# Routed experts in fp32: two plain layers against seven-product block multiplication with the next expert's first layer ahead

## The chip, the cores and the metric

The kernel runs on one core of a Trainium2 chip. The metric is the device time of one execution in microseconds (us). It is the median of three runs, 475.67 us for the kernel before (475.49 to 475.71). Engines are called PE (TensorE matmul), PEld (TensorE weight load), DVE (VectorE), ACT (ScalarE), POOL (GpSimd) and SP (SyncE, which issues the weight loads).

## What is computed

A recurrent attention block gives a 384-vector for each of 3072 tokens. A router picks one of eight experts per token, and each expert is a two-layer network on its own tokens:

```python
for e in range(E):                       # E = 8
    mask = expert_idx == e
    h = np.maximum(x[mask] @ w1[e], 0.0) # w1[e]: 384 x 1024
    out[mask] = gate_w[mask, None] * (h @ w2[e])   # w2[e]: 1024 x 384
```

Everything is float32. The change is in these two products; attention and routing stay as they are.

## The kernel before

**Up to 205 us: attention and routing.** Attention, router and token lists run under a manual schedule: each engine executes its instructions in the order of the program text (`attention`, from L713). Experts are ranked by load. The two lightest ranks, 7 and 6 (`LAST`, L34), are settled early. Their first 128 tokens are computed during the end of attention by the class `Early` (L804), so they have only 256 tokens left.

**From 205 us: the experts, in the order `TURN`** (L35), that is ranks 7, 6, 0, 1, 2, 5, 4, 3. Their token counts are the capacities `CAPS` (L32), less the 128 done early: 256, 256, 448, 416, 416, 384, 384, 384. Each expert goes through `expert` (L903) in these steps:

- Token rows have been gathered by indirect DMAs on the POOL queue (L887) into a ring of eight buffers. PE transposes them, 3 per tile of 128 tokens (L912), and DVE copies the result from PSUM into `xT` (L915).
- Layer 1 (L920): 8 blocks of 128 hidden units, 3 blocks of the 384 inputs, so 24 matmul calls of N columns, N being the expert's token count. ACT applies the ReLU out of PSUM (L921).
- Layer 2 has two forms. With a token count divisible by 128 it makes 8 matmul calls of 384 columns per tile (L938). With 416 or 448 it computes the transposed output by 24 calls of N columns (L928), ACT copies it (L929), and PE transposes it back (L935).
- DVE multiplies by the gate out of PSUM (L940), and POOL scatters the rows to the output by an indirect DMA (L941).

The core of it:

```python
for f in range(NF):                                   # NF = 8
    ps = k.ps.tile([128, TM * 128], F32, name="ps", tag="ps")
    for m in range(NK):                               # NK = 3
        mm(ps[:, 0:n], w1[:, m, f * 128 : (f + 1) * 128], xT[:, m, 0:n], start=(m == 0), stop=(m == NK - 1))
    nc.scalar.activation(hT[:, f, 0:n], ps[:, 0:n], ACT.Relu)
...
        for f in range(NF):
            mm(ps, hT[:, f, at], w2[:, f, :], start=(f == 0), stop=(f == NF - 1))
    y = k.gp.tile([128, DM], F32, name="y", tag="y", bufs=4)
    nc.vector.tensor_scalar_mul(y[0:here], ps[0:here], gate[0:here])
    nc.gpsimd.indirect_dma_start(
```

In the trace one float32 matmul call is two MATMUL records with a weight load each: the 192 calls of L920 are 384 records.

**What sets the order.** The expert part stands outside the manual schedule (L1098 to L1105), so the framework's scheduler orders it. Weights have two buffers per layer; the load for the expert two places ahead is issued by SP after each expert (L1104, L1105, through L237 and L245, L246), and starts when the buffer is free. [...] All waits between engines are semaphores that the framework puts in.

Of the kernel before, what the change touches and what calls it, by code (L numbers as in the profile page):

```python
# [9 lines left out]
F32 = mybir.dt.float32  # L10
# [16 lines left out]
TM = 4  # L27
# [199 lines left out]
    yield  # L227


def weight_tiles(k):  # L230
    return (
        k.wp.tile([128, NK, F], F32, name="w1", tag="w1"),
        k.wp.tile([128, NF, DM], F32, name="w2", tag="w2"),
    )


def load_weights_of(k, s, tiles):  # L237

    e = k.nc.sync.value_load(k.who[0:1, s : s + 1], min_val=0, max_val=E - 1)
    load_weights(k, e, tiles)  # L240


def load_weights(k, e, tiles):
    w1, w2 = tiles
    k.nc.sync.dma_start(out=w1, in_=k.w1[bass.ds(e, 1)].rearrange("o (c p) f -> p (o c) f", p=128))  # L245
    k.nc.sync.dma_start(out=w2, in_=k.w2[bass.ds(e, 1)].rearrange("o (f p) m -> p (o f) m", p=128))  # L246


def load(k, i, other=None):
# [293 lines left out]
def put(k, g, b):  # L543

    t0 = (g.c * B + b) * C
    k.nc.sync.dma_start(out=k.xs[t0 : t0 + C, :], in_=g.X[:, b, :])
# [166 lines left out]
def attention(k):  # L713


    units = B * NCH

    def on(f, i):
        if 0 <= i < units:
            f(k, i)  # L720

    def of_group(f, i):
        if 0 <= i < units:
            f(k, k.groups[i // B], i % B)

    def whole(f, i):
        if 0 <= i < units and i % B == B - 1:
            f(k, k.groups[i // B])

    emb = build_experts(k)  # L730
    for i in range(-1, units + 7):
        j = i - SETTLED * B
        if 0 < i + AHEAD < units:
            load(k, i + AHEAD)
        if i < 2:
            next(emb)
        whole(summed, i - 6)
        whole(places, i - 4)
        on(own_rows, i)
        on(turn, i + 1)  # L740
        on(scaled, i + 2)
        on(own, i + 1)
        on(states, i)
        of_group(squares, i - 1)
        whole(choose, i - 3)
        whole(listed, i - 5)
        if j == 10:
            k.lists = turned_lists(k, perm, "st")
            lists = taken_by_rank(k, k.lists)
            first = [Early(k, r, *lists, w) for r, w in zip(LAST, k.weights)]  # L750
        on(sums, i)
        on(carry, i)
        on(scores, i + 1)
        on(rows, i)
        of_group(put, i)
        on(own_sum, i + 1)
        of_group(turn_rows, i - 1)
        of_group(logits, i - 2)
        whole(ranks, i - 3)
        whole(gates, i - 3)  # L760
        if i == units:
            first[0].hidden(0)
        whole(taken, i - 5)
        if i == B:
            decays(k)
        if i == 2:
            build_turned(k)
        if 3 <= i < 3 + len(k.ring):
            k.nc.gpsimd.memset(k.ring[i - 3], 0.0)
        if j == 7:  # L770
            load_, count = loads(k, "st")
        if j == 8:
            settle(k, load_, count)
            for w, r in zip(k.weights, LAST):
                load_weights_of(k, r, w)
        if j == 9:
            perm = turner(k, k.by)
        if j == 10:
            to = outs(k, lists[0], E * TM)
        if i == units - 1:  # L780
            for f in first:
                f.turn()
        if i == units + 1:
            first[0].hidden(1)
        if i == units + 2:
            first[0].rows(0)
        if i == units + 4:
            first[0].rows(1)
            load_, _ = loads(k, "lg")
            first[0].out(to)  # L790
            first[1].hidden(0)
    by = order(k, load_, k.settled)
    lists = turned_lists(k, turner(k, by), "lg")
    first[1].hidden(1)
    k.take, k.gates = taken_by_rank(k, lists)
    k.rows_of = {r: gathers(k, r) for r in LAST}
    k.to = outs(k, k.take, E * TM)
    first[1].rows(0)
    first[1].rows(1)
    first[1].out(to)  # L800
    caps_passed(k, load_, by)
# [80 lines left out]
def gather(k, take, to, gate, n=128):  # L882

    nc = k.nc
    G = k.ring[k.turns % len(k.ring)]
    k.turns += 1
    nc.gpsimd.indirect_dma_start(  # L887
        out=G[0:n, :], out_offset=None, in_=k.xs[:, :], in_offset=IndirectOffsetOnAxis(ap=take[0:n], axis=0),
        bounds_check=N - 1, oob_is_err=False,
    )  # L890
    return G, to, gate, n


def gathers(k, r):

    return [
        gather(k, k.take[:, j : j + 1], j, k.gates[:, j : j + 1], min(128, CAPS[r] - t))
        for t, j in zip(range(0, CAPS[r], 128), range(r * TM, (r + 1) * TM))
        if t > 0 or r not in LAST
    ]  # L900
# [43 lines left out]
        )  # L944


def all_lists(k):

    nc = k.nc
    with ExitStack() as ctx:  # L950
        attention_pools(k, ctx)
        slots = numbers(k, "allslots", [128, SLOTS], [[1, SLOTS]], 0, 0)
        sums = k.ps.tile([128, 2, SLOTS], F32, name="allsums", tag="y")
        for c in range(NCH):
            lane, what = slices(k, c, slots)
            for b in range(B):
                i = c * B + b
                nc.tensor.matmul(
                    sums.rearrange("p q s -> p (q s)"), lane[:, b, :], what[:, b].rearrange("p q s -> p (q s)"),
                    start=(i == 0), stop=(i == NCH * B - 1),  # L960
                )
        take = tiles(k, sums, SLOTS)
        to = outs(k, take, SLOTS)
        gate = k.const.tile([128, SLOTS], F32, name="allgates")
        nc.vector.tensor_copy(gate, sums[:, 1, :])
        nc.sync.dma_start(out=k.list.rearrange("e p t -> p e t"), in_=take.rearrange("p (e t) -> p e t", e=E))
        nc.sync.dma_start(out=k.tlist.rearrange("e p t -> p e t"), in_=to.rearrange("p (e t) -> p e t", e=E))
        nc.sync.dma_start(out=k.glist.rearrange("e p t -> p e t"), in_=gate.rearrange("p (e t) -> p e t", e=E))
# [80 lines left out]
@with_exitstack  # L1049
def kernel(  # L1050
    ctx: ExitStack,
    tc: tile.TileContext,
    r: bass.AP,
    k: bass.AP,
    v: bass.AP,
    w: bass.AP,
    u: bass.AP,
    moe_expert_emb: bass.AP,
    moe_tau: bass.AP,
    moe_w1: bass.AP,  # L1060
    moe_w2: bass.AP,
    out: bass.AP,
):
    assert tuple(r.shape) == (B, H, S, D) and tuple(out.shape) == (N, DM)
    assert tuple(moe_w1.shape) == (E, DM, F)
    n = Net()
    n.tc, n.nc = tc, tc.nc
    n.r, n.k, n.v, n.w, n.u = r, k, v, w, u
    n.emb, n.tau, n.w1, n.w2, n.out = moe_expert_emb, moe_tau, moe_w1, moe_w2, out
    nc = n.nc  # L1070

    def pool(name, bufs, **kw):
        return ctx.enter_context(tc.tile_pool(name=name, bufs=bufs, **kw))

    n.const = pool("const", 1)
    n.wp = pool("wp", 2)
    n.xs = tc.dram_tile([N, DM], F32, name="xs")
    n.list = tc.dram_tile([E, 128, TT], I32, name="list")
    n.tlist = tc.dram_tile([E, 128, TT], I32, name="tlist")
    n.glist = tc.dram_tile([E, 128, TT], F32, name="glist")  # L1080
    n.x_dram = tc.dram_tile([128, S, D // 4], F32, name="x_dram")
    n.need_dram = tc.dram_tile([E, TG], I32, name="need_dram")

    n.Rpad, n.Kpad, n.state = [], [], []
    for name in ("loaded", "KU", "diag", "xd", "RT", "KT", "AT", "st", "y", "groups"):
        setattr(n, name, {})
    n.weights = [weight_tiles(n) for _ in range(2)]
    with ExitStack() as ctx1, tc.manual_schedule():
        n.aconst = ctx1.enter_context(tc.tile_pool(name="aconst", bufs=1))
        n.io = ctx1.enter_context(tc.tile_pool(name="io", bufs=AHEAD + 2))  # L1090
        attention_pools(n, ctx1)
        build_first(n)
        for i in range(1, AHEAD - 1):
            load(n, i)
        build_consts(n)
        attention(n)

    with ExitStack() as ctx2:  # L1098
        expert_pools(n, ctx2)
        for i, r in enumerate(TURN):  # L1100
            rows = n.rows_of.pop(r) if r in LAST else gathers(n, r)
            expert(n, [(G, n.to[:, j : j + 1], gate, here) for G, j, gate, here in rows], *n.weights.pop(0))
            if i + 2 < E:
                n.weights.append(weight_tiles(n))  # L1104
                load_weights_of(n, TURN[i + 2], n.weights[-1])  # L1105
    again(n)


# [26 lines left out]
```

## Time and profile before

| | us |
|---|---|
| median of 3 runs (range) | 475.67 (475.49 to 475.71) |
| the profiled execution, its own time | 475.24 |
| its span, first to last instruction | 473.4 |
| PE busy | 447.4 (95%) |
| DVE, ACT, POOL busy | 148.8, 138.2, 171.7 |
| the first transposes of the experts | 205.31 |
| the end of the last expert's matmuls | 462.1 |
| L920, L938, L928, PE busy | 120.9, 67.9, 52.0 |

The experts take 256.8 us of the span. Start times on PE, in us from the start of the span:

| rank (tokens) | transposes L912 | layer 1 L920 | layer 2 L938 or L928 |
|---|---|---|---|
| 7 (256) | 205.31 | 206.32 | 216.78 |
| 6 (256) | 227.10 | 228.31 | 238.78 |
| 0 (448) | 249.09 | 251.08 | 269.22 |
| 1 (416) | 288.76 | 291.15 | 308.01 |
| 2 (416) | 326.24 | 328.63 | 345.50 |
| 5 (384) | 363.73 | 366.08 | 381.67 |
| 4 (384) | 397.15 | 398.48 | 414.07 |
| 3 (384) | 429.55 | 430.89 | 446.47 |

How to read the profile: the groups by line give count, busy time and mean duration of one record. Successive matmuls overlap, so a record's duration (486 ns for 384 columns) is longer than the step from one start to the next; the pace is read from the timeline. A release line such as "[0.42 <-DVE xTe L915]" says how long the engine stood idle and which instruction ended that.

### The profile page before, as it was taken

To read this page: it belongs to the slowest core of one execution; us is meant where nothing else is said; L and a number is where in the kernel's file an instruction comes from. 1 tells how busy PE (TensorE), PEld (TensorE's weight loads), DVE (VectorE), ACT (ScalarE), POOL (GpSimd) and SP (SyncE) were. 2 spreads that over 40 slices of the span, in tenths; PEclk is the share of its full clock that TensorE was granted. 3 is DMA by queue.
4 is the path that set the end of the run, shared out by engine and by line. 5 is a ranking of instruction groups with operands and counts; after the bars stand their busy time and mean duration, and the time that the engine had idled before them with its cause. 6 is when DMAs were issued, how large, how long until landed. Compare 5 with 4: busy or idle time off the path is not lost.

```text
span 473.4 us, 7292 instructions
## 1 busy us (share of the span) xinstructions
PE 447.4 (95%) x2716; PEld 317.5 (67%) x2716; DVE 148.8 (31%) x416; ACT 138.2 (29%) x410; POOL 171.7 (36%) x260
## 2 busy tenths in 40 slices
PE   8789999999999889999999999999998999999990
PEld 3578889898989778866765555555555555556550
DVE  4556776566657754230102003003002002011010
ACT  2376655665565561101101201201210200201200
POOL 7766677665856433360204003303301201011010
PEclk9999999999999999999999999999999999999996
DMA  8766645654561393143535125134232243100000
GB/s 177 141 135 136 134 95 108 135 127 106 105 135 35 106 406 123 47 138 133 184 150 200 27 106 198 57 133 149 103 133 87 113 151 120 46 18 32 1 37 19
DMA packets 93791, 54.26 MB, mean 115 GB/s; under 512 B 76937, under 2 KB 88380, under 8 KB 93746
## 3 DMA queue, kind: packets, MB, share of 16 engines
q1 hardware_dynamic: 89024, 43.85, 33.6%
q0 software_dynamic: 3296, 9.44, 5.6%
q10 hardware_dynamic: 1426, 0.41, 0.4%
q8 instruction: 23, 0.38, 0.3%
q14 instruction: 22, 0.18, 0.1%
HBM read 44.45 MB, written 9.63 MB: 114 GB/s over the span
## 4 chain that ended last, share of the span: by engine, by line
PE 79%; DVE 9%; ACT 4%; SPq 2%; issue 2%; DMA 2%; POOL 1%; POOLq 0%; ACTq 0%; DVEq 0%
PE ps L920 26%; PE ps L938 14%; PE ps L928 11%; PE at L322 5%; PE y L372 3%; PE y L369 3%; PE st L339 3%; PE early_h L834 2%; DVE AT L326 2%; ACT xd L294 2%; PE lg L491 2%; PE early_y L845 2%; PE yrows L394 2%; DVE y L940 1%; PE kt L309 1%
## 5 line engine op out<-in xcount | busy, mean ns | idle before, releaser
L920 PE MATMUL ps<-xTe,w 128*128 128x384 f32 (+3 forms) x384 | 120.9, 475 | 3.0 <-DVE xTe L915 2.8
L920 PEld LDWEIGHTS ps<-xTe,w 128*128 128x128 f32 x384 | 72.3, 190 | 48.3 <-issue 22.3
L941 POOL DMA_INDIRECT out_dram<-y,to x25 | 24.7, 987 | 205.0 <-DVE y L940 186.7
L940 DVE TENSOR_SCALAR y<-ps,gates 128x384 f32<-128x384 f32 (+2 forms) x25 | 14.6, 613 | 229.4 <-PE ps L938 125.2
L921 ACT ACTIVATE hT<-ps 128x384 f32<-128x384 f32 (+3 forms) x64 | 30.2, 478 | 165.3 <-PE ps L920 165.2
L938 PE MATMUL ps<-w,hT 128*128 128x384 f32 x208 | 67.9, 486 | 0.0
L938 PEld LDWEIGHTS ps<-w,hT 128*128 128x128 f32 x208 | 39.5, 190 | 27.1
L928 PE MATMUL ps<-hT,w 128*128 128x416 f32 (+1 forms) x144 | 52.0, 521 | 0.0
L294 ACT ACTIVATE xd<-V,diag 128x48 f32<-128x48 f32 x192 | 45.8, 321 | 19.3 <-DVE diag L286 14.9
L928 PEld LDWEIGHTS ps<-hT,w 128*128 128x128 f32 x144 | 27.4, 190 | 24.2 <-issue 24.2
L326 DVE TENSOR_TENSOR AT<-at,umask 128x512 f32<-128x512 f32 x48 | 30.9, 686 | 34.2 <-PE at L322 34.2
L322 PE MATMUL at<-RT,KT 48*128 48x128 f32 x384 | 27.9, 285 | 4.4 <-ACT KT L311 3.4
L356 POOL TENSOR_TENSOR state<-state,wpow 48x192 f32<-48x192 f32 x40 | 20.4, 511 | 28.0 <-DVE state L352 26.5
L887 POOL DMA_INDIRECT G<-xs,take x25 | 25.2, 1008 | 12.2 <-issue 5.8
L322 PEld LDWEIGHTS at<-RT,KT 48*128 48x128 f32 x384 | 23.3, 187 | 9.3 <-ACT KT L311 5.1
L372 PE MATMUL y<-AT,V 128*48 128x128 f32 x384 | 25.9, 277 | 0.0
L280 POOL TENSOR_TENSOR KU<-KU,Rpad 128x384 f32<-128x384 f32 x24 | 24.1, 1003 | 1.9
L271 POOL TENSOR_TENSOR Kpad<-K,kpow 128x384 f32<-128x384 f32 x23 | 23.1, 1003 | 3.3 <-DVE kpow L100 2.0
L279 POOL TENSOR_TENSOR KU<-K,u_bc 128x384 f32<-128x384 f32 x24 | 24.1, 1003 | 0.3 <-DVE diag L286 0.3
L372 PEld LDWEIGHTS y<-AT,V 128*48 128x48 f32 x384 | 19.8, 122 | 3.0
L369 PE MATMUL y<-RT,state 128*112 128x128 f32 x160 | 21.2, 275 | 0.0
L478 ACT COPY xT<-xp 128x384 f32<-128x384 f32 x24 | 11.5, 480 | 31.3 <-PE xp L476 31.3
(183 smaller groups left out, 515.1 us busy)
## 6 DMA issues: line engine op xcount, KB each, us to landing
w<-in_moe_w_dram SPq DMA_DIRECT2D x16, 1536.0 KB, 6.3
K<-in_k_dram SPq DMA_DIRECT2D x24, 192.0 KB, 3.6
V<-in_v_dram SPq DMA_DIRECT2D x24, 192.0 KB, 3.5
xs<-X SPq DMA_DIRECT2D x24, 192.0 KB, 2.0
Rpad<-in_r_dram SPq DMA_DIRECT2D x23, 192.0 KB, 3.6
G<-xs,take POOLq DMA_INDIRECT x27
out_dram<-y,to POOLq DMA_INDIRECT x25
Rpad<-in_r_dram ACTq DMA_DIRECT2D x1, 192.0 KB, 4.0
```

The costliest lines, as they stand in the source:

```text
L279: nc.gpsimd.tensor_mul(KU, K, k.u_bc)
L294: k.nc.scalar.mul(xd[:, h, :], V[:, h, :], diag[:, h : h + 1])
L322: nc.tensor.matmul(at[s][:, p, :], KT[rows, p, :], RT[rows, p, :], start=True, stop=True)
L326: nc.vector.tensor_mul(a, at[s], k.umask[:, None, :].to_broadcast([128, NP, C]))
L369: mm(y[0:PP, p, :], T[:, p, 0:PP], RT[:, p, :], start=(p == 0), stop=False, skip_group_check=True)
L372: mm(y[s * DP : s * DP + D, p, :], V[:, 2 * p + s, :], AT[s][:, p, :], start=(c == 0 and p == 0), stop=True, skip_group_check=True,)
L887: nc.gpsimd.indirect_dma_start(out=G[0:n, :], out_offset=None, in_=k.xs[:, :], in_offset=IndirectOffsetOnAxis(ap=take[0:n], axis=0), bound ...
L920: mm(ps[:, 0:n], w1[:, m, f * 128 : (f + 1) * 128], xT[:, m, 0:n], start=(m == 0), stop=(m == NK - 1))
L921: nc.scalar.activation(hT[:, f, 0:n], ps[:, 0:n], ACT.Relu)
L928: mm(ps[:, 0:n], w2[:, f, m * 128 : (m + 1) * 128], hT[:, f, 0:n], start=(f == 0), stop=(f == NF - 1))
L938: mm(ps, hT[:, f, at], w2[:, f, :], start=(f == 0), stop=(f == NF - 1))
L941: nc.gpsimd.indirect_dma_start(out=k.out[:, :], out_offset=IndirectOffsetOnAxis(ap=to[0:here], axis=0), in_=y[0:here, :], in_offset=None, ...
```

## The change

Both layers are computed with Strassen's block products, all in one manual order. For a 2 by 2 block product seven block multiplications replace eight, at the price of sums of blocks before and after.

- **Layer 1** (`Block.hidden`), all experts but the first: the blocks are two of the three input blocks, two halves of the hidden units and two halves of the tokens. The third input block is added plainly. The sums of weights `Sw` (`weigh`) are made by DVE and POOL, two each, 128x512; those of tokens `Tx` (in `turn`) by DVE, four of 128 by half the token count; those of products by DVE and ACT. The first expert's layer 1 stays plain (`plain`).
- **Layer 2** (`Block.out`), first 256 tokens: two token tiles, two halves of the hidden units, two halves of the 384 outputs. The sums of hidden values `Sh` (`halves`) are four DVE operations of 128x512, those of the weights `Tw` (`weigh_out`) four POOL operations of 128x768. Tokens after the 256th go through `rest`, which is as before.
- **Order** (`experts`): per step the halves of expert i, layer 1 of expert i+1, weight sums for i+2, then layer 2 of expert i with the transposes of i+2 before its rest, then gathers for i+3, `weigh_out` for i+1 and the load of w2 for i+2. ACT, not DVE, copies the transposed rows. The attention pools are closed before the expert pools open, inside the manual schedule.

`...` marks what is left out.

```diff
+class Block:
...
+    def turn(self):
...
+            nc.scalar.copy(self.xT[:, m, 0:n], ps[:, 0:n])
+        if self.rank != TURN[0]:
+            b = [[self.xT[:, m, s * n // 2 : (s + 1) * n // 2] for s in range(2)] for m in range(2)]
+            self.T = [k.xtp.tile([128, TM * 64], F32, name=f"Tx{j}", tag=f"Tx{j}")[:, 0 : n // 2] for j in range(4)]
+            combined(nc.vector, nc.vector, *self.T, b[0][0], b[0][1], b[1][0], b[1][1])
+    def weigh(self):
...
+        summed_up(nc.gpsimd, nc.vector, *self.S, a[0][0], a[1][0], a[0][1], a[1][1])
+    def weigh_out(self):
...
+        combined(nc.gpsimd, nc.gpsimd, *self.T, b[0][0], b[0][1], b[1][0], b[1][1])
...
+    def hidden(self):
...
+        def add(ps, weights, f, moving, first=False):
+            for j in range(2):
+                nc.tensor.matmul(
+                    ps[:, j, :], weights[:, (f + j) * 128 : (f + j + 1) * 128], moving,
+                    start=(first and j == 0), stop=True, skip_group_check=True,
+                )
...
+        for f in range(0, NF // 2, 2):
+            g = f + NF // 2
+            p1, p6, p5, p7 = bank(), bank(), bank(), bank()
+            add(p1, w1[:, 0, :], f, x[:, 0, one], first=True)
+            p1s = kept("p1")
+            nc.scalar.copy(p1s, p1)
+            add(p6, self.S[1], f, self.T[1], first=True)
+            u2 = kept("u2")
+            vec.tensor_add(u2, p6, p1s)
+            add(p5, self.S[0], f, self.T[0], first=True)
+            p15 = kept("p15")
+            vec.tensor_add(p15, p5, p1s)
+            add(p7, self.S[2], f, self.T[2], first=True)
+            p157 = kept("p157")
+            vec.tensor_add(p157, p7, p15)
+            add(p1, w1[:, 1, :], f, x[:, 1, one])
+            add(p1, w1[:, 2, :], f, x[:, 2, one])
+            nc.scalar.activation(self.hT[:, f : f + 2, one], p1, ACT.Relu)
+            add(p5, self.S[3], f, x[:, 1, two])
+            add(p5, w1[:, 2, :], f, x[:, 2, two])
+            vec.tensor_add(self.hT[:, f : f + 2, two], p5, u2)
+            relu(f, two)
+            add(p7, w1[:, 1, :], g, self.T[3])
+            add(p7, w1[:, 2, :], g, x[:, 2, one])
+            vec.tensor_add(self.hT[:, g : g + 2, one], p7, u2)
+            relu(g, one)
+            add(p6, w1[:, 2, :], g, x[:, 2, two])
+            vec.tensor_add(self.hT[:, g : g + 2, two], p6, p157)
+            relu(g, two)
+    def halves(self):
...
+        summed_up(nc.vector, nc.vector, *self.S, a[0][0], a[0][1], a[1][0], a[1][1])
+    def out(self, between):
...
+        add(p1, h[:, lo, 0:128], w2[:, lo, half], first=True)
+        nc.scalar.copy(p1s, p1)
+        add(p6, S[1], T[1], first=True)
+        vec.tensor_add(u2, p6, p1s)
+        nc.scalar.mul(u21, u2, gate[1])
+        nc.scalar.mul(u20, u2, gate[0])
+        add(p5, S[0], T[0], first=True)
+        nc.scalar.mul(p5s, p5, gate[1])
+        add(p7, S[2], T[2], first=True)
+        vec.scalar_tensor_tensor(u3, p7, gate[1], u21, ALU.mult, ALU.add)
+        vec.tensor_add(y[1][:, other], u3, p5s)
+        add(p7, h[:, hi, 128:256], T[3])
+        vec.scalar_tensor_tensor(y[1][:, half], p7, gate[1], u21, ALU.mult, ALU.add)
+        self.put(1, y[1])
+        add(p1, h[:, hi, 0:128], w2[:, hi, half])
+        nc.scalar.mul(y[0][:, half], p1, gate[0])
+        add(p5, S[3], w2[:, hi, other])
+        vec.scalar_tensor_tensor(y[0][:, other], p5, gate[0], u20, ALU.mult, ALU.add)
+        self.put(0, y[0])
+        between()
+        if self.n > 256:
+            self.rest(self.n - 256)
...
+def combined(eng, other, t1, t2, t3, t4, b11, b12, b21, b22):
+    eng.tensor_sub(t1, b12, b11)
+    other.tensor_sub(t3, b22, b12)
+    eng.tensor_sub(t2, b22, t1)
+    eng.tensor_sub(t4, b21, t2)
+def summed_up(eng, other, s1, s2, s3, s4, a11, a12, a21, a22):
+    other.tensor_add(s1, a21, a22)
+    eng.tensor_sub(s2, s1, a11)
+    other.tensor_sub(s3, a11, a21)
+    eng.tensor_sub(s4, a12, s2)
+def experts(k):
...
+    for b in blocks[0:2]:
+        b.gather()
+        b.turn()
+    blocks[1].weigh()
+    blocks[0].plain()
+    first_weights(2)
+    blocks[2].gather()
+    blocks[0].weigh_out()
+    for i in range(E):
+        blocks[i].halves()
+        for b in at(i + 1):
+            b.hidden()
+        for b in at(i + 2):
+            b.weigh()
+        first_weights(i + 3)
+        blocks[i].out(lambda: [b.turn() for b in at(i + 2)])
+        for b in at(i + 3):
+            b.gather()
+        for b in at(i + 1):
+            b.weigh_out()
+        second_weights(i + 2)
...
-    with ExitStack() as ctx2:
+        ctx1.close()
         expert_pools(n, ctx2)
-        for i, r in enumerate(TURN):
-            rows = n.rows_of.pop(r) if r in LAST else gathers(n, r)
-            expert(n, [(G, n.to[:, j : j + 1], gate, here) for G, j, gate, here in rows], *n.weights.pop(0))
-            if i + 2 < E:
-                n.weights.append(weight_tiles(n))
-                load_weights_of(n, TURN[i + 2], n.weights[-1])
+        for name, bufs in (("cb", 1), ("ev", 2)):
+            setattr(n, name, ctx2.enter_context(tc.tile_pool(name=name, bufs=bufs)))
+        experts(n)
     again(n)
```

`add` in `out` is four matmul calls, one per 128 hidden units of a half, with 192 moving columns.

## Prediction

> **What bounds the kernel now.** I read the page's busy shares and chain first, then the timeline of the experts, single lines, and the granted clock in windows of 1 us.
>
> ```profile
> PE 447.4 (95%) x2716; PEld 317.5 (67%) x2716; DVE 148.8 (31%) x416; ACT 138.2 (29%) x410; POOL 171.7 (36%) x260
> ...
> PE 79%; DVE 9%; ACT 4%; SPq 2%; issue 2%; DMA 2%; POOL 1%; POOLq 0%; ACTq 0%; DVEq 0%
> ```
>
> PE carries 79% of the chain, and no other engine is busy for half of the span. In the experts PE is nearly alone on the chain (timeline of one 384-token expert: start, length, engine, instruction):
>
> ```profile
> 398.48 15.75 PE L920 MATMUL ps<-xTe,w 128*128 128x384 f32 x48 [0.19 <-DVE xTe L915]
> 400.78 0.49 ACT L921 ACTIVATE hT<-ps 128x384 f32<-128x384 f32 x1 [18.43 <-PE ps L920]
> 402.66 0.49 ACT L921 ACTIVATE hT<-ps 128x384 f32<-128x384 f32 x1 [1.38 <-PE ps L920]
> 404.59 0.49 ACT L921 ACTIVATE hT<-ps 128x384 f32<-128x384 f32 x1 [1.44 <-PE ps L920]
> 414.07 15.64 PE L938 MATMUL ps<-w,hT 128*128 128x384 f32 x48
> 429.55 1.15 PE L912 MATMUL ps<-ident,G 128*128 128x128 f32 x9
> ```
>
> Six records of 384 columns pass between two ReLUs: 1.93 us, so 0.322 us each. The ReLUs of the other experts come every 2.255 us (448), 2.095 (416) and 1.295 (256): 0.376, 0.349, 0.216. All four fit N/1.2 + 2.5 ns per record.
>
> Do narrow matmuls keep this, or does the weight load (190 ns a record) set their pace? The early experts have 128 columns (timeline of the weight loads):
>
> ```profile
> 193.25 2.76 PEld L834 LDWEIGHTS early_h<-earlyx,w 128*128 128x128 f32 x24
> ```
>
> 24 loads take 2.76 us, one each 112 ns: loads overlap, and only at 128 columns (109 by the fit) do they bind. From 160 columns on columns count.
>
> The change puts large element-wise work on POOL beside DVE, so I looked for both in one stretch:
>
> ```profile
> 157.87 1.01 POOL L279 TENSOR_TENSOR KU<-K,u_bc 128x384 f32<-128x384 f32 x1 [0.33 <-DVE diag L286]
> 158.21 0.69 DVE L630 TENSOR_SCALAR settled<-by 128x8 f32<-128x8 f32 x1
> 158.81 0.20 DVE L646 TENSOR_TENSOR eq<-by,number 1x64 f32<-1x64 f32 x1
> 158.95 1.00 POOL L280 TENSOR_TENSOR KU<-KU,Rpad 128x384 f32<-128x384 f32 x1
> 159.05 0.97 DVE L650 TENSOR_TENSOR is_e<-eq,number 1x64 f32<-1x64 f32 x1
> ```
>
> L650 has two SBUF inputs of 64 elements; its other execution took 0.211 us. Here it took 0.97 and ended at 160.02, with POOL's L280 (159.95). L630 ended with L279. DVE operations with a PSUM input (L306, 0.68 us) keep their time beside POOL.
>
> [...] The trace shows the fall, 2 us after the last matmul; it doesn't show the return (window, PE busy, PEld, DVE, ACT, POOL, granted clock, DMA share, GB/s):
>
> ```profile
> 462.00:463.00 1.00, 0.11 (x1) 0.00 (x0) 0.62 (x1) 0.00 (x0) 0.00 (x0) 1.00 0.00 0
> 463.00:464.00 1.00, 0.00 (x0) 0.00 (x0) 0.00 (x0) 0.00 (x0) 0.95 (x1) 1.00 0.03 8
> 464.00:465.00 1.00, 0.00 (x0) 0.00 (x0) 0.00 (x0) 0.00 (x0) 0.01 (x1) 0.58 0.43 169
> ```
>
> **PE work removed and added.** In us, with the fit, two records a call; 0.112 at 128 columns.
>
> Before: layer 1 is 48 records an expert: 2x10.36 (256), 18.04 (448), 2x16.76 (416), 3x15.48 (384), sum 118.7. Layer 2: 2x10.32, 18.04, 2x16.76, 3x15.48, sum 118.6. Transposes 75+36 at about 0.12 (L912, nine in 1.15): 13.3. Sum 250.6 of the 256.8 us from 205.31 to 462.1; 6.2 is idle.
>
> After: first layer 1 plain 10.36; then 88 records of half the tokens: 9.86 (128), 16.65 (224), 2x15.47 (208), 3x14.3 (192). Layer 2: 56 records of 192 columns at 0.1625, 9.1 for each of eight, 72.8. Rest: 7.8, 2x6.52, 3x5.16, sum 36.3. Transposes 75+18: 11.2. Sum 231.0. So there is room for 25.8 us of stalls before the change loses. The seven products save only 19.6 us because a third of layer 1 and the tokens after the 256th stay plain.
>
> **New stalls of PE**, by the queues in their written order. Step i is round i of the loop in `experts`: halves of block i, layer 1 of block i+1, layer 2 of block i. A call is two records.
>
> 1. *Layer 2, p7 read and accumulated at once.* In `out` the second half of p7 follows the first directly, and u3 reads p7 between them. So PE waits for its own last record to land and for DVE:  PE's slot end to DVE's start is 0.20 (L938 ends 397.15, L940 starts 397.35), 192 columns 0.35 (L352), return 0.05: 0.6, eight times, 5.0.
>
> 2. *`halves` ahead of layer 1's evictions on DVE.* Behind the rest of one block PE issues 12 calls of the next `hidden` (p1, p6, p5, p7, p1 twice); the 13th adds to p5, which DVE must have read for p15. DVE first has the last gate product (0.2+0.62), four halves at about 0.65 (L326 and L559: 0.69 alone), u2 and p15 (0.5 each): 4.35 us, against 12 calls of 0.325 = 3.9 (384) or 4.2 (416). For steps 3, 4, 5: 0.3, 0.65, 0.65. At steps 1 and 2 the 256-token block before has no rest to hide the token sums `Tx`: PE waits some 0.4 for their t2 ahead of p6, and 0.3 for p15. Sum 3.0. Later evictions hide: six of 0.55 (L398) are 3.3 us of DVE against 22 calls of 0.325, 7.15 us of PE; if DVE took twice as long they would set the pace.
>
> 3. *Transposed rest*, three experts: two transposes (0.25) stand between the last matmul and the need of its ACT copy (0.2+0.35): 0.3 each, 0.9.
>
> 4. *Step 0.* POOL's queue: early scatter to 206.5, two weight sums after DVE's to 212.7, four gathers at 1.3 (L887 on the timeline) to 217.9, then `weigh_out` without a gap. PE ends `plain` at 217.3; the last ReLU is 0.6 later, so `halves` starts at 217.9 too. Each has two SBUF inputs. Without exclusion p15 is read at 221.3, and PE, ready at 219.95, loses 1.35. A POOL operation of 768 elements: 1.003 at 384, 0.401 at 128, slope 2.35 ns, so 1.95 us. The trace doesn't show who goes first when both wait for each other; I take turns, so that three POOL operations fall between four halves: 1.35+5.85 = 7.2. Bounds: none (1.35; a gain is excluded, as the halves themselves remain), four ahead (9.2). Behind the waiting halves on DVE stand all evictions of layer 1, and PE waits for those.
>
> 5. *Step 6*, no gathers left: POOL reaches `weigh_out` 2.1 us after PE's end of the rest. One or two halves wait: 2.5 (bounds 0.45 and 4.5).
>
> 6. *Step 7* has no layer 1. PE issues four calls (1.3) and needs t2, POOL's third operation after the last scatter. First half s3 (to 2.8), t1 to 4.75, s4 to 5.4, t3 and t2 to 9.3: PE loses 8.05. Without exclusion 2.1+5.85-1.3 = 6.65. Most of this is the order's own cost: no other work lies between.
>
> 7. *Clock.* Idle stretches of 7 and 8 us in 4 and 6 halve it. [...]
>
> Sum: 5.0+3.0+0.9+7.2+2.5+8.05+4.0 = 30.7. PE ends at 205.3+231.0+30.7 = 467.0 in place of 462.1: +4.9. The tail (L940, L941, end) stays. On the profiled execution, 475.24: 480.1; the median lies 0.43 above it: **480.5**.
>
> **What is hidden.** POOL's `weigh_out` in steps 2 to 4: scatter, second scatter 3.4 us behind the first (L941: 298.84, 302.23), three gathers, then t2 at 15.1 us after the rest; PE needs it at 16.25. If that cover fails each 0.1 us per POOL operation beyond it costs 0.3. On SP the two loads of an expert are apart now, each at the place where its buffer comes free; they land in 6.3 us, a step of 30 us ahead. Gathers are moved ahead of `weigh_out` on POOL, 3.9 to 5.2 us a step, which is in the times above. Row copies go to ACT, which has room (five of 0.49 per 7.15 us). `weigh` delays u2 by 2 us behind 3.9 us of PE: nothing. Its two POOL sums, 1.3 each, end before the first scatter.
>
> **Rivals.**
>
> - *Faster: exclusion scarcely falls on PE's path.* If `halves` wins the race of step 0, stalls 4 to 6 fall to 1.35+0.45+6.65, and the clock drops once: 5.0+3.0+0.9+8.45+2.0 = 19.4, so 6.4 us gained: 469.2. For it: start times in 4 are within 1 us. Against: L650. It decides at 25.8 us, about three waits of 1.95 fewer than I count.
> - *Slower: waits cost PE by themselves.* The trace has a PE-queue EVENT_SEMAPHORE of 51 ns at some waits (L834, L920). Seven layers of 22 adds and eight of 7 are 210 places: 10.7 us, so 491. Against: L920 keeps its fitted pace past waits for PSUM banks.
> - *It doesn't do what it says: weight loads of 190 ns set narrow matmuls.* 760 records of 192 columns lose 0.0275, 176 of 208 lose 0.014, 96 of 160 lose 0.054, 88 of 128 lose 0.078: 35 us, so 515. L834 speaks against it.
>
> **Chances.** Forecast case (476.7 to 488): 0.58. Faster rival, 467 to 474.7: 0.25. Between, within 0.2% (what a measurement can tell): 0.07. Semaphores 0.08, weight loads 0.02. Bounds of 4 to 7 give -8 (no waits, no drops) to +12 (9.2, 4.5, 8.05, 7), so 468 to 488; semaphores stay out.
>
> **What would show it.** Step 0: PE idle ahead of p5's second accumulation, DVE's `halves` records of 2 us or more beside POOL's. Step 7: PE idle for 8 us until the third `weigh_out`. A gap of 0.6 us in each layer 2. Records of 192 columns 0.163 us apart; the experts' matmul time near 220 us. Half clock after the two long gaps. Wrong if POOL's 768 elements take over 2.3 us (t2 late in every step), [...] or if PE stalls inside `hidden`.

## The result and the profile after

The changed kernel takes 494.68 us (median of 4 runs, 493.2 to 498.18) against 475.58 for the kernel before on the same chip: 1.0413 times as long, 95% interval 1.0357 to 1.0469. The forecast was 480.5 with a range of 468 to 488, so the sign was right and the time lay outside the range. The profiled execution took 494.1 us, with a span of 491.8. PE ends the experts at 480.68 instead of 462.11, 18.57 us later, which is the whole difference of the spans (18.4); the tail behind it is 11.1 us, 11.3 before.

Below, "stretch" is the time on PE from the experts' first transposes to the end of the last matmul. It is the cleaner measure, because the attention stage ends anywhere from 204.7 to 207.8 us in the profiled executions. It was 256.80 us before and is 275.16 after (205.52 to 480.68).

From the page of the changed kernel: busy times, and the two PE groups that waited longest.

```profile
PE 437.6 (89%) x3266; PEld 393.5 (80%) x3266; DVE 258.3 (53%) x574; ACT 169.2 (34%) x488; POOL 254.6 (52%) x306
...
L1094 PE MATMUL ps<-Tw,Sh 128*128 128x192 f32 x192 | 34.4, 338 | 9.2 <-POOL Tw L1164 9.2
...
L1032 PE MATMUL ps<-xTe,Sw 128*128 128x192 f32 (+3 forms) x56 | 13.2, 362 | 16.3 <-DVE p L1052 16.3
```

DVE and POOL gained 110 and 83 us of busy time, and part of DVE's is waiting, as step 0 shows below. PE waits 16.3 us for `p15` (L1052, behind the `halves` on DVE's queue) and 9.2 us for t2 (L1164, POOL's third sum). The chain of waits is of no use here: followed back from the end it breaks off at a DMA at 453.97.

**Pace.** Narrow matmuls run as forecast (timeline, layer 1 of 384 tokens):

```profile
358.38 2.11 PE L1032 MATMUL ps<-Tx,Sw 128*128 128x192 f32 x12
...
360.33 1.46 PE L1032 MATMUL ps<-xTe,w 128*128 128x192 f32 x8
...
361.63 0.81 PE L1032 MATMUL ps<-xTe,Sw 128*128 128x192 f32 x4
```

Twelve records in 1.95 us and eight in 1.30 are 0.1625 us each, the value of the fit. The 48 records of 160 columns from 377.58 take 6.53 us, 0.136 each, which is the fit's value too; twelve of 128 columns from 232.60 take 1.34, 0.112 each, as the early experts' weight loads did. PE's work shrank as worked out; what grew is waiting.

Steps are rounds of the loop in `experts`, as in the prediction. A "half" is one of the four DVE sums of `halves`, L1170 to L1173; t1 to t4 are POOL's four sums `Tw`, issued in the order t1, t3, t2, t4, L1162 to L1165.

**Step 0.** Timeline of the changed kernel around the start of `halves`:

```profile
217.25 1.83 POOL L1162 TENSOR_TENSOR Tw<-w 128x768 f32<-128x768 f32 x1
...
217.87 5.29 DVE L1170 TENSOR_TENSOR Sh<-hT 128x512 f32<-128x512 f32 x1 [6.82 <-ACT hT L1014]
...
219.03 1.81 POOL L1163 TENSOR_TENSOR Tw<-w 128x768 f32<-128x768 f32 x1
...
220.80 1.80 POOL L1164 TENSOR_TENSOR Tw<-w,Tw 128x768 f32<-128x768 f32 x1
222.67 2.14 POOL L1165 TENSOR_TENSOR Tw<-w,Tw 128x768 f32<-128x768 f32 x1
223.19 2.17 DVE L1171 TENSOR_TENSOR Sh<-Sh,hT 128x512 f32<-128x512 f32 x1
...
227.38 1.19 PE L1032 MATMUL ps<-xTe,Sw 128*128 128x128 f32 x4 [7.29 <-DVE p L1052]
```

The first half takes 5.29 us where an undisturbed one takes 0.69. It waits not for one POOL operation but for three (t1, t3, t2), and gets in ahead of the fourth (t4, L1165, whose 2.14 us in place of 1.8 hold its wait for DVE). The second half then waits for t4. PE stands for 7.3 us.

**Step 6.** The same lines at the last layer 1:

```profile
419.71 0.69 DVE L1171 TENSOR_TENSOR Sh<-Sh,hT 128x512 f32<-128x512 f32 x1
420.31 6.10 DVE L1172 TENSOR_TENSOR Sh<-hT 128x512 f32<-128x512 f32 x1
420.53 1.82 POOL L1162 TENSOR_TENSOR Tw<-w 128x768 f32<-128x768 f32 x1
...
425.94 2.14 POOL L1165 TENSOR_TENSOR Tw<-w,Tw 128x768 f32<-128x768 f32 x1
426.34 2.28 DVE L1173 TENSOR_TENSOR Sh<-hT,Sh 128x512 f32<-128x512 f32 x1
...
429.70 1.62 PE L1032 MATMUL ps<-xTe,Sw 128*128 128x192 f32 x4 [7.38 <-DVE p L1052]
```

Two halves got through before POOL came; the third lost 5.4 us to three sums and the fourth 1.6 to t4. PE is idle from 422.15 to 429.70, 7.55 us, in a step forecast at 2.5. In step 7 PE waits 6.35 us for t2.

**Clock.** Windows (length, busy PE, PEld, DVE, ACT, POOL, granted clock, DMA share, GB/s) of the step-0 gap and its end:

```profile
222.00:223.00 1.00, 0.00 (x0) 0.00 (x0) 1.00 (x1) 0.00 (x0) 0.92 (x2) 0.66 1.00 414
...
228.00:229.00 1.00, 1.00 (x6) 1.00 (x6) 0.00 (x0) 0.00 (x0) 0.00 (x0) 0.50 0.09 16
...
232.00:233.00 1.00, 1.00 (x8) 1.00 (x8) 0.42 (x1) 0.56 (x3) 0.00 (x0) 0.72 0.00 0
```

The clock halves inside the gap, and after PE resumes at 227.38 it stays half until about 232.6: 5.2 us, of which half, some 2.6, is lost. The gaps of steps 6 and 7 are followed by 4.3 and 2.9 us of work at half clock.

### The profile page after: what moved, and what is told of

The parts are those of the page before. It is cut to its first block, busy times and chain, and to the rows that moved or that the text cites. A ratio compares the mean times of both kernels' runs of the same rounds, so it can differ in the third digit from the quotient of the medians.

```text
span 491.8 us, 8850 instructions
## 1 busy us (share of the span) xinstructions
PE 437.6 (89%) x3266; PEld 393.5 (80%) x3266; DVE 258.3 (53%) x574; ACT 169.2 (34%) x488; POOL 254.6 (52%) x306
## 5 line engine op out<-in xcount | busy, mean ns | idle before, releaser
L1032 PE MATMUL ps<-xTe,w 128*128 128x192 f32 (+3 forms) x336 | 65.4, 336 | 0.0
L1032 PEld LDWEIGHTS ps<-xTe,w 128*128 128x128 f32 x336 | 58.5, 200 | 0.5
L1094 PE MATMUL ps<-Tw,Sh 128*128 128x192 f32 x192 | 34.4, 338 | 9.2 <-POOL Tw L1164 9.2
L1094 PEld LDWEIGHTS ps<-Tw,Sh 128*128 128x128 f32 x192 | 32.7, 197 | 10.4 <-POOL Tw L1164 10.4
L1039 ACT ACTIVATE hT<-hT 128x384 f32<-128x384 f32 (+3 forms) x42 | 22.0, 523 | 54.5 <-DVE hT L1061 39.9
L1032 PE MATMUL ps<-Tx,Sw 128*128 128x192 f32 (+3 forms) x168 | 29.8, 327 | 0.0
L1032 PEld LDWEIGHTS ps<-Tx,Sw 128*128 128x128 f32 x168 | 27.7, 191 | 0.2
L1032 PE MATMUL ps<-xTe,Sw 128*128 128x192 f32 (+3 forms) x56 | 13.2, 362 | 16.3 <-DVE p L1052 16.3
L1171 POOL TENSOR_TENSOR Sw<-Sw,w 128x512 f32<-128x512 f32 x7 | 11.4, 1631 | 24.2 <-DVE Sw L1170 16.2
L1094 PE MATMUL ps<-w,hT 128*128 128x192 f32 x128 | 23.4, 326 | 0.0
```

The source lines that it names most:

```text
L1032: nc.tensor.matmul(ps[:, j, :], weights[:, (f + j) * 128 : (f + j + 1) * 128], moving, start=(first and j == 0), stop=True, skip_group_che ...
L1039: nc.scalar.activation(h, h, ACT.Relu)
L1094: nc.tensor.matmul(ps, a[:, f, :], b[:, f, :], start=(first and f == 0), stop=(f == NF // 2 - 1), skip_group_check=True)
```

## Experiments

Theory: POOL's four sums of w2 cost almost all of the loss. DVE operations with two SBUF inputs wait beside them (the exclusion of the prediction; halves of 5.29 and 6.10 us above, 0.69 undisturbed), and t2 comes late (6.35 us in step 7). Rivals: waits cost PE by themselves; or layer 1's many DVE sums are the burden.

The runs were made on several chips. Each ratio is to the kernel before on the same chip (medians from 475.51 to 477.53 us); kernels of different experiments are best compared by the stretch.

**1. Without POOL's sums.**

```diff
-        combined(nc.gpsimd, nc.gpsimd, *self.T, b[0][0], b[0][1], b[1][0], b[1][1])
+        self.T = [b[0][1], b[1][1], b[1][0], b[0][0]]
```

> Leaves out the four POOL sums of w2 in every expert: quadrants of w2 stand in for them, so the output is not the reference's. Theory (DVE's halves are locked out while POOL's sums run, and PE waits for sums that come late): halves take 0.7 us each, the gaps of steps 0 and 6 fall from 7.4 and 7.5 to 1.4 and 0.6, no wait for Tw in steps 3, 4, 5 and 7 (3.5 and 6.4), no half clock (6.3): 29 us less, about 465.5. Rival (the chain of DVE work is itself too long, whatever POOL does): the gaps of steps 0 and 6 stay, only the waits for Tw go with the clock loss after the last: about 483.

465.82 us, 0.979 of before (0.9747 to 0.9832). Halves take 0.68 to 0.69 each, the gaps at steps 0 and 6 fall to 1.21 and 0.36, and the stretch to 246.36. The sums alone turn 2% of gain into 4% of loss, 28.8 us of stretch. The number of adds into PSUM, with their semaphores, is the same, so waits as such are not the cause; nor are layer 1's DVE sums, which this kernel keeps.

**2. When does DVE get in?** Two orders of the same four sums. First each sum behind the one it reads:

```diff
+    eng.tensor_sub(t1, b12, b11)
+    eng.tensor_sub(t2, b22, t1)
+    eng.tensor_sub(t4, b21, t2)
+    eng.tensor_sub(t3, b22, b12)
```

> Order of POOL's four sums t1, t2, t4, t3 in place of t1, t3, t2, t4, so that the second and third depend on the one just before. Theory ([...] DVE gets in only where one waits for the last): step 6 lets DVE in after t1 and after t2, its gap falls from 7.5 to about 4.4; t2 comes one place earlier, so steps 3 to 5 lose 3.5 and step 7 about 1; step 0 about the same: 8 us less, about 486.5. Rival (DVE and POOL take turns at every operation): steps 0 and 6 unchanged, only t2 earlier, about 489.5.

488.62 us, 1.0262 (1.0198 to 1.0327). Timeline of step 6:

```profile
419.17 2.60 DVE L1179 TENSOR_TENSOR Sh<-hT 128x512 f32<-128x512 f32 x1
419.38 1.82 POOL L1169 TENSOR_TENSOR Tw<-w 128x768 f32<-128x768 f32 x1
...
421.28 2.14 POOL L1170 TENSOR_TENSOR Tw<-w,Tw 128x768 f32<-128x768 f32 x1
...
425.05 1.62 PE L1032 MATMUL ps<-xTe,Sw 128*128 128x192 f32 x4 [3.88 <-DVE p L1052]
```

The half now waits for one sum, not three: 2.60 in place of 6.10 us. POOL's t2 starts 0.08 us after t1 ends, and DVE takes that pause. Reading t1 is not enough: t2 does so in the changed kernel too, but with t3 in between, and there DVE did not get in ahead of it. The gap of step 6 halves to 3.88 and that of step 7 falls to 4.90, since t2 comes second; step 0 stays at 7.0, because all four halves wait there. In steps 4 and 5 PE now waits for t3, the last sum (1.55 and 1.35 us); the expectation had these steps free of waits, and the time is 2 us above it.

Then the reverse, no sum reading another:

```diff
+    eng.tensor_sub(t1, b12, b11)
+    eng.tensor_sub(t3, b22, b12)
+    eng.tensor_sub(t2, b22, b11)
+    eng.tensor_sub(t4, b21, b22)
```

> The changed kernel, except that POOL's four sums of the second layer's weights no longer read one another: t2 = b22 - b11 and t4 = b21 - b22 stand in for t2 = b22 - t1 and t4 = t2 - b21, so part of the result is wrong; the count, the size and the place of POOL's operations are those of the changed kernel. Theory (VectorE's reads wait through a train of POOL operations for as long as each starts on the heels of the one before, and get in at the pause that an operation makes when it waits for the result of the one before): without such pauses the third half of the hidden layer waits for the whole train in step 6, about 7.9 us for that one record in place of 6.10, and the first half of step 0 takes about 7 us in place of 5.29; PE's gaps at steps 0, 6 and 7 stay near 7.5, 7.5 and 6.3 us, and the time stays at 494 to 495 us. Rival (what decides is not the dependence but a fixed stretch of POOL work, or VectorE's turn coming by itself): the records stay at 5.3 and 6.1 us, each with one of about 2.2 us after it. A second rival: independent operations alternate with VectorE's from the start, records of about 2.2 us, and the gap of step 6 falls to about 3 us, the time to about 489 us.

495.17 us, 1.0393 (1.0351 to 1.0435). Step 6:

```profile
419.45 7.86 DVE L1179 TENSOR_TENSOR Sh<-hT 128x512 f32<-128x512 f32 x1
...
424.95 1.80 POOL L1172 TENSOR_TENSOR Tw<-w 128x768 f32<-128x768 f32 x1
427.23 0.68 DVE L1180 TENSOR_TENSOR Sh<-hT,Sh 128x512 f32<-128x512 f32 x1
...
428.98 1.62 PE L1032 MATMUL ps<-xTe,Sw 128*128 128x192 f32 x4 [7.53 <-DVE p L1052]
```

The half waits for all four sums, 7.86 us against the 7.9 expected (step 0: 7.05), and the fourth half is free. PE's gap is the same, because the same four sums stand ahead of it. So for these sums the dependence of one on the one just before decides when DVE gets in; both rivals on record fall.

One thing stays open. In the chain at step 0, DVE also got in between t4 and the independent t3, after t4 had itself had to wait (2.13 us). In the next experiment, step 0's sums early, the independent t1 and t3 alternate with DVE's operations (2.22 and 2.25 us each), t1 having found DVE at work. In both cases the turns followed a POOL operation that had itself waited (2.13 and 2.22 us in place of 1.8); no run isolates this.

**3. The sums out of the way.** First, only step 0's go ahead of the second expert's `weigh`:

```diff
+    blocks[0].weigh_out()
     blocks[1].weigh()
     blocks[0].plain()
     first_weights(2)
     blocks[2].gather()
-    blocks[0].weigh_out()
```

> The first expert's POOL sums go ahead of the weight sums and gathers, so that they run beside its plain first layer. Lock-out theory: gap of step 0 from 7.4 to about 1.4 us and its half clock gone (2.5): 8.5 us less, about 486. Rival of a DVE chain too long by itself: step 0 unchanged, about 494.7.

487.55 us, 1.024 (1.0194 to 1.0286). Step 0's gap falls to 1.80 us (1.35 was the estimate without exclusion); those of steps 6 and 7 stay at 7.39 and 6.19. The stretch is 8.04 us shorter: 5.5 of gap, and 2.5 that agree with the clock's 2.6.

Second, all the later sums: a second buffer for `Tw`, and `weigh_out` for the next expert ahead of this one's layer 2.

```diff
-        self.T = [... name=f"Tw{j}", tag=f"Tw{j}") for j in range(4)]
+        self.T = [... name=f"Tw{j}", tag=f"Tw{j}", bufs=2) for j in range(4)]
...
         first_weights(i + 3)
+        for b in at(i + 1):
+            b.weigh_out()
         blocks[i].out(lambda: [b.turn() for b in at(i + 2)])
...
-        for b in at(i + 1):
-            b.weigh_out()
```

> Second buffer for the sums of w2, and they are issued ahead of the layer 2 of the expert before, not after it. Lock-out theory: steps 3 to 5 lose their waits for Tw (3.5 us), step 6 its gap (7.0), step 7 falls from 6.4 to about 1 us, half clock after both gone (3.8): 19.7 us less, about 475; step 0 keeps its 7.4. Rival of a DVE chain too long by itself: step 6 keeps its gap, about 484.

475.02 us (11 runs), 0.9976 (0.9952 to 1.0001). The gaps of steps 6 and 7 are 0.41 and 0.83 us, PE never waits for a weight sum, and step 0 keeps its 7.30. The stretch is 20.17 us shorter: 12.3 of gaps at 6 and 7, 3.5 of late t2 in steps 3 to 5, and the rest, about 4.3, is mostly the two drops of the clock (4.3 and 2.9 us at half speed, 3.6 lost).

**4. p7's second half behind p1's and p5's.** The three lines from `add(p7, h[:, hi, 128:256], T[3])` to `self.put(1, y[1])` move to just ahead of `between()`.

> In layer 2 the second half of p7 moves behind those of p1 and p5, so that DVE can read its first half meanwhile. If PE waits there for that read, eight gaps of 0.85 us go: 6.8 us less, about 488. If the gap is only where PE waits for something that is late anyway (rival), it moves to the next product and the time stays at 494.7.

491.70 us, 1.032 (1.0287 to 1.0353). All eight waits for L1110 (5.4 us in the list of waits) are gone, and the stretch is 7.03 us shorter, 0.88 for each layer 2. The time fell by 3.0 only. In the profiled execution the experts began 2.1 us later, which is the attention stage's doing, and the tail behind PE grew from 11.1 to 13.7 us, which is the edit's. In the last expert the first scatter now goes out at 470.48, each scatter waits for the one before to land, and the last starts 2.6 us behind PE's end, 0.9 before the edit. None of my expectations had counted that.

**5. The load of w2 a few microseconds later.** In steps 3 to 5 PE also waited for t2: 0.15, 1.6 and 1.76 us. Timeline of the changed kernel, from the end of step 3 to the wait of step 4:

```profile
349.05 0.37 SPq L252 DMA_DIRECT2D w<-in_moe_w_dram  x1
...
350.57 1.69 POOL L1154 DMA_INDIRECT out_dram<-y,to  x1 [6.39 <-DVE y L1149]
...
357.46 0.92 POOL L1154 DMA_INDIRECT out_dram<-y,to  x1 [5.20 <-DMA out_dram<-y,to]
...
367.78 2.38 PE L1094 MATMUL ps<-Tw,Sh 128*128 128x192 f32 x13 [1.44 <-POOL Tw L1164]
```

The second scatter starts 6.9 us after the first, waiting for the first to land, while SP's w2 load fills the DMA engines (share 0.97 and 1.08 in the windows from 351 to 355). The gathers and sums queue behind it. The edit puts that load into the next step:

```diff
         first_weights(i + 3)
+        if i > 0:
+            second_weights(i + 1)
...
-        second_weights(i + 2)
```

> The load of w2 for expert i+2 is issued after the first-layer load of the next step, some 15 us later. Theory (the scatters of the transposed rest are 6 to 7 us apart because the 1.5 MB load runs beside them, so the gathers and the sums on POOL come late): the second scatter follows after about 3.4 us, no wait for Tw in steps 3, 4, 5, 3.5 us less, about 491. Rival (the scatters wait for one another at that distance anyway): distance and time unchanged, 494.7.

493.04 us, 1.0354 (1.0318 to 1.039). At the same place:

```profile
350.51 1.68 POOL L1154 DMA_INDIRECT out_dram<-y,to  x1 [5.07 <-DVE y L1149]
354.55 0.92 POOL L1154 DMA_INDIRECT out_dram<-y,to  x1 [2.37 <-DVE p L1052]
```

The distance falls to 4.0 us, at a DMA share of 0.13 and 0.11 in the windows from 351 to 355, and step 4's wait for t2 is gone; step 5 keeps 1.13. There SP has no first-layer load left ahead of the w2 load, which by the order of its queue can start as early as in the changed kernel (an estimate). In that kernel all three such pairs start behind a w2 load (issued at 314.22, 349.05 and 384.40) and are 6.4, 6.9 and 7.1 us apart. So the load is the cause of the distance. The gain, 1.4 us of stretch, is small, and the intervals of the ratios overlap. PE's waits for t2 fell by 2.2 us, but after the gap of step 7 the matmuls kept half their pace for 5.9 us, in place of 2.9.

**6. The repairs of 3 and 4 together.**

> The first expert's sums early, the sums of w2 ahead of layer 2 with a second buffer, and p7 last. If the losses add, 475.0 less 8 (step 0 and its half clock) less 6.8 (p7): about 460. If the products need the stalls anyway (rival: PE waits move to other places), above 468.

463.38 us, 0.972 (0.9688 to 0.9752), faster than both kernels. The single savings add to 35.2 us of stretch (8.04, 20.17, 7.03); together they save 32.9. What remains, from its list of waits on PE:

```profile
PE ps L1032 <- DVE p L1052: 3.7, 6, 1.8
...
PE ps L1032 <- DVE Tx L1164: 1.5, 2, 0.9
```

**7. The tail given back.** The last expert alone keeps p7's second half in its old place:

```diff
+        if last:
+            second_of_p7()
         add(p1, h[:, hi, 0:128], w2[:, hi, half])
...
+        if not last:
+            second_of_p7()
```

> The three repairs together, but the last expert keeps p7's second half ahead of p1's and p5's. With p7 behind, the first two scatters of the last expert start late, each waits for the one before to land, and the last scatter starts 2.6 us after PE's end, in place of 0.9. Theory (that is why the end behind PE grew from 11.1 to 13.3 us): the end falls back to 11 to 11.3 us, the stretch grows by one wait of 0.9 us to about 243.2, and the time is 1 to 1.7 us below the three repairs, about 462. Rival (the longer end has another cause, or the order of the scatters only shifts it): the end stays near 13.3 us and the time is 463.4 to 464.3.

463.03 us (6 runs), 0.972 (0.9686 to 0.9755). The last scatter, first in experiment 6 (PE ends at 448.42), then here (447.95):

```profile
451.02 0.97 POOL L1154 DMA_INDIRECT out_dram<-y,to  x1 [2.67 <-DMA out_dram<-y,to]
```

```profile
448.88 0.97 POOL L1162 DMA_INDIRECT out_dram<-y,to  x1 [3.60 <-DVE y L1157]
```

It waits for its data again and no longer for the scatter ahead. The tail is 11.2 us in place of 13.2, the stretch 243.21 in place of 242.30: 1.1 us better between the experts' start and the end, as the theory had it. The medians, and the ratios, do not tell the two kernels apart.

**8. What each part is worth.** The new order with plain products; then the repaired kernel with only layer 1, or only layer 2, in products.

> The new fixed order, with the next expert's first layer ahead, but plain products in both layers and none of the sums. PE's work is then that of the kernel before (250.6 us) with next to no idle: if its idle of 6 us was from the order, about 471. If the order by itself costs (rival), above 475.6.

> The version with all three repairs, but only layer 1 by products; layer 2 is plain and its sums are gone. By PE's work: 8.4 us less than the order with plain products (475.1), some 2 us of it given back in waits for token sums: about 468.5; the experts' stretch 248 us. If the products of layer 1 cost as much in waits as they save (rival): 475.

> The version with all three repairs, but only layer 2 by products; layer 1 is plain and DVE has none of its sums. By PE's work: 9.5 us of matmuls and 2.2 us of transposes less than the order with plain products, about 1 us given back at the end: about 464.5, within 2 us of both layers together; the experts' stretch 243.5 us. If DVE's halves and POOL's sums meet again (rival), above 468.

| kernel | median us | ratio to before (95%) | stretch us |
|---|---|---|---|
| order alone | 475.07 | 0.9959 (0.9924 to 0.9994) | 254.27 |
| order, layer 1 in products | 469.24 | 0.9835 (0.9797 to 0.9873) | 248.03 |
| order, layer 2 in products | 464.41 | 0.9742 (0.9698 to 0.9785) | 242.62 |
| both | 463.38 | 0.972 (0.9688 to 0.9752) | 242.30 |

The two kernels with one layer in products ran on another chip than the other two. The order alone shortens the stretch by 2.5 us, and its time stays well above the 471 expected. Layer 2's products save 11.65 us of stretch over the order alone. Layer 1's save 6.2 alone, but only 0.3 on top of layer 2's. The windows over each whole stretch, first layer 2 only, then both:

```profile
205.71:448.33 242.62, 241.28 (x1117) 185.66 (x1117) 42.62 (x96) 59.00 (x137) 106.01 (x78) 1.00 0.33 111
```

```profile
206.12:448.42 242.30, 235.65 (x1397) 221.94 (x1397) 117.93 (x222) 66.32 (x151) 126.36 (x92) 1.00 0.33 111
```

Layer 1's products take 5.6 us off PE's busy time (241.28 to 235.65) and give 5.3 back as idle time (1.34 to 6.65): the waits for `p15` and `Tx` shown under 6, 5.2 us. DVE, at 118 us in place of 43, is half idle over the stretch, but it is late at each change from one expert to the next. In the kernel with layer 1's products alone no halves stand ahead of `p15`: PE does not wait for it there, and 1.0 us for `Tx`.

## Why the prediction fell short

The forecast stretch was 231.0 of work and 30.7 of stalls, 261.7; measured 275.16. By the numbered items of the prediction:

| item | forecast us | measured us |
|---|---|---|
| work of PE | 231.0 | 232.1 |
| 1, p7 read and accumulated | 5.0 | 7.0 |
| 2, `halves` ahead of evictions | 3.0 | 3.1 |
| 3, transposed rest | 0.9 | 1.1 |
| 4, step 0 | 7.2 | 7.45 |
| 5, step 6 | 2.5 | 7.55 |
| 6, step 7 | 8.05 | 6.35 |
| 7, clock | 4.0 | 6.3 |
| "What is hidden": t2 in steps 3 to 5 | 0 | 3.5 |

The measured column adds to 274.5; 0.7 is unassigned. PE's work is 231.0 by the pace, which held, and 1.1 more of transposes: twelve take 1.9 to 2.0 us, in both kernels, where I had 0.12 each from a row of nine.

- **Item 5, step 6, failed most, by 5.05 us, and with its upper bound.** It took one or two halves to wait for one sum each, 4.5 at worst. POOL arrived about when forecast, 2.3 us after the end of the rest; the length of the wait was wrong. The turns were an estimate of mine that no trace had shown. What came in their place: a half of DVE waited for the whole train of POOL operations (7.86 us for four in experiment 2), or until one had to wait for the result of the one before (6.10 us in the changed kernel, behind three, and 2.60 in the chain, behind one). L650 in the trace of before could not tell: it began inside L280 and so shows the wait for one POOL operation, not for a train.
- **Item 4, step 0, came out right by luck, with a wrong mechanism.** It had three halves wait for one sum each. In fact two halves waited through what was left of four sums, 6.1 us together. The same mechanism is what item 5 missed.
- **Item 6, step 7, named the right wait**, PE for t2. But each sum took 1.80 us, not 1.95, and t2 did not have to wait for a half, as turn-taking had it: 6.35 lies near the item's own figure without exclusion, 6.65.
- **The cover of t2, put at no cost, failed by an overlooked row.** 3.4 us between scatters was read at 298.84, where no load ran. The same trace has 289.31 to 295.46, 6.15 us, behind a w2 load issued at 287.46; this is the case that the change meets in its later steps. I had taken loads on SP as free because they land early, and had asked only for their landing.
- **Item 1 was mis-sized.** The wait itself is 0.68, near the 0.6; the stretch of experiment 4 gives 0.88 a time. What the other 0.2 is, no run shows.
- **Item 7.** Three long gaps, not two, halved the clock. The forecast's 4.0, 2.0 lost for each gap, like the 2.0 of its faster rival, was an assumption: the trace of before shows the fall of the clock, not its return. Here 5.2, 4.3 and 2.9 us passed at half clock, so 2.6, 2.2 and 1.5 were lost. The time at half pace did not go with the length of the gap: step 7's 6.2 us of waiting was followed by 2.9 us here and by 5.9 in experiment 5.
- **Right:** the pace of narrow matmuls, layer 2's saving (9.5 of products and 2.1 of transposes forecast, 11.65 measured), item 3, and the direction. Item 2 held in its sum only: no wait for token sums came at steps 1 and 2. The rival of semaphores is out by experiments 1 and 6, that of weight loads by the pace. Exclusion did fall on PE's path, so the faster rival fell for this kernel; a kernel in which it scarcely does (experiment 6) gained 13.3 us on its chip (476.64 to 463.38).
- **Slips in its sums, too small to matter:** eight times 0.6 is 4.8, not 5.0; item 2's terms add to 4.42, not 4.35; the line through 0.401 and 1.003 us gives 1.91 for 768 elements, not 1.95; and 2.1 of the 19.6 us saved are transposes, not products.

## What to carry to other kernels

Fewer multiplications pay only if the sums that replace them lie where nobody waits: name for every sum the engine that runs beside it and the moment at which its result is needed, above all at the first and last round of a loop, where the covering work is missing. Where a DVE operation with two SBUF inputs meets back-to-back POOL sums, count the whole train as DVE's wait, not one operation (here 4.6 and 5.4 us for three sums, 6.4 and 7.2 for four). Before such a scheme is spread over two layers, measure each alone and on top of the other: layer 1's products saved 6.2 us of stretch alone and 0.3 beside layer 2's.

## What the runs showed of the hardware

- In the changed kernel a POOL train of three sums held off a two-input DVE operation for 4.6 us (step 0) and 5.4 (step 6), with the sums independent a train of four for 6.4 (step 0) and 7.2 (step 6). Where a sum read the one just before it, it started 0.07 to 0.08 us behind it and DVE got in (t4 at 222.67 in the changed kernel, t2 at 421.28 in the chain).
- A small DVE operation waited too: in the kernel with step 0's sums early, L1248, one element with two SBUF inputs, took 1.75 us beside a POOL sum; in the kernel before, where no POOL sum ran beside it, the same operation (L977) took 0.15.
- DVE operations with one PSUM and one SBUF input kept their time beside POOL's sums: in the chain L1049 and L1052 took 0.55 and 0.54 us inside t4's 423.50 to 425.63; without the sums (experiment 1) the same two take 0.56 and 0.55.
- An indirect scatter that waits for the one before it started 6.4 to 7.1 us behind it beside a weight load and 4.0 without; in the tail, with no load, 3.4 to 4.2.
- In the changed kernel PE's idle gaps of 7.45, 7.55 and 6.35 us halved its granted clock (0.50), and 5.2, 4.3 and 2.9 us of work passed before it was full again. In the other kernels, where the timelines show the matmuls behind gaps of 4.0 to 7.6 us, they run at half pace for some 3 to 6 us. The 4.0 is step 6 in the kernel of the chained sums; there it took 4.9.
